# Five forms of the large products, each tried in one block or one chunk

## The chip, the cores and the metric

The kernel runs on one core of a Trainium2 chip. The metric is device time in microseconds (us) from start to end of one launch; less is better. The engines are TensorE (PE, with its weight loads shown apart as PEld), VectorE (DVE), ScalarE (ACT), GpSimd (POOL) and SyncE (SP), which issues most DMAs.

## The reference

Sliding-window attention (8 batches, 8 heads, 576 positions, head size 64, window 128, a linear distance bias), then a feed-forward pair over all 4,608 tokens: 512 to 2,048, Relu, square, 2,048 to 512.

```python
scores = scale * q @ k^T ; where(0 <= rel < 128, scores + bias, -1e9)
attn = exp(scores - max) ; attn / (sum + 1e-9) ; x = attn @ v
h = np.maximum(x @ w_in, 0.0)
return (h * h @ w_out).astype(np.float32)
```

## The kernel before

The 4,608 tokens are cut into `NCH` = 9 chunks of 512. For each chunk `c` the feed-forward part runs over `NF` = 16 slices `f` of 128 hidden units. A slice has two blocks of twelve products: `gemm1(c, f)` writes a [128 hidden x 512 tokens] bank `g`, and `gemm2(c, f)` adds into the four banks `acc[0..3]` ([128 outputs x 512 tokens] each), which are written out after `f` = 15. That is 9 x 16 x 24 = 3,456 large products of 128 x 128 weights by 512 columns.

Precision comes from a split: every f32 operand is kept as a high and a low part of type fp32r, and a product is made of three, high by high, high by low, low by high. The weights of a slice live in one area of 8 KB a partition, in which the high and the low word of a weight lie side by side (`[.., 512, 2]`, line 157). `block` (L177) picks 128 weights of one part, so a plain weight load reads every second word. Where `APART` holds (gemm1, every fourth `f`, first two of four blocks) the order in memory is another one, and the load reads every fourth word. The moving operand of gemm1 is `x[c, p]`, a tile `xu` of [128, 2, 512]: the 512 high words stand together, then the 512 low words. That of gemm2 is `hh` and `hl`, each 512 words together. Every product carries its own weight load.

Behind gemm1 there is a chain per block: ACT Relu out of bank `g` into `r` (L204), DVE square (L207), ACT cast to `hh` (L211), DVE subtraction to `hl` (L213). gemm2 of that slice comes two slices later.

Attention of the later chunks runs in pairs of heads (`Couple`), one pair per four slices: between the blocks TensorE takes the score products (L392, 64-row tiles) and the value products (L338, tiles with 64 columns of weights, into the bank `at`), and `high` and `low` (L477, L480) write the result as the two parts of `xu`. The first chunk's attention (`Wide`, L508, L544, L547) and the conversion of all weights (`convert`, L161: ACT scale, two DVE passes, a cast, a DVE subtraction) fill a prologue of some 37 us and run on into chunk 0.

The order on TensorE is the order of the program: even steps hold gemm1, odd steps gemm2 of two slices before, and the attention pieces stand ahead of every fourth odd step. In the first part a planner (`Plan`) with written costs places all engines' steps; afterwards the engines other than TensorE are ordered by the tile framework, with some steps raised in priority.

Of the kernel before, what the change touches and what calls it, by code (L numbers as in the profile page):

```python
# [9 lines left out]
F32 = mybir.dt.float32  # L10
F32R = mybir.dt.float32r
BF16 = mybir.dt.bfloat16
I32 = mybir.dt.int32
AF = mybir.ActivationFunctionType
ALU = mybir.AluOpType
# [7 lines left out]
NF = DF // 128  # L23
# [14 lines left out]
FIRST = 39  # L38
APART = lambda i, f, b: i == 0 and f % 4 == 0 and b < 2
CASTS = (0, 2, 15,)  # L40
COPIES = (3,)
SQUARES = (6,)
NORMS = (7,)
# [18 lines left out]
class Kern:  # L62
# [98 lines left out]
    def convert(self, f):  # L161
        nc = self.nc
        lo, hi = self.raw[f][..., 0], self.raw[f][..., 1]
        flo, fhi, wl, wh = lo.bitcast(F32), hi.bitcast(F32), self.w[f][..., 0], self.w[f][..., 1]
        nc.scalar.activation(fhi, fhi, AF.Prelu, scale=2.0**-112, alpha=2.0**32)  # L165
        yield
        nc.vector.tensor_scalar(lo, lo, 29, None, op0=ALU.logical_shift_right)
        yield
        nc.vector.scalar_tensor_tensor(lo, hi, 3, lo, op0=ALU.logical_shift_left, op1=ALU.bitwise_or)
        yield  # L170
        (nc.gpsimd.tensor_copy if f in CASTS else nc.scalar.copy)(wh, flo)
        yield
        nc.vector.tensor_tensor(wl, flo, wh.bitcast(F32), op=ALU.subtract)
# [3 lines left out]
    def block(self, i, f, b):  # L177
# [5 lines left out]
            w = w[:, 128 * b : 128 * b + 128]  # L183
        return w[..., 0], w[..., 1]

    def gemm1(self, c, f):
        nc = self.nc
        xs = [self.x[c, p] for p in range(NP)]
        g = self.g1.tile([128, 512], F32, name="g")
        i = 0  # L190
        for cc in range(NCC):
            wl, wh = self.block(0, f, cc)
            for w, part in ((wh, 0), (wh, 1), (wl, 0)):
                nc.tensor.matmul(g, w, xs[cc][:, part], start=i == 0, stop=i == 11)  # L194
                i += 1
                if (c, f, i) == (0, 0, 9):
                    yield
        yield
        r = self.hp.tile([128, 512], F32, name="r", bufs=1)
        hh = self.hp.tile([128, 512], F32R, name="hh")  # L200
        hl = self.hp.tile([128, 512], F32R, name="hl")
        self.h[c, f] = hh, hl
        with self.tc.high_priority(offset=100):
            self.relu = nc.scalar.activation(r, g, AF.Relu)  # L204
        yield
        if c or f in SQUARES:
            nc.vector.tensor_tensor(r, r, r, op=ALU.mult)  # L207
        else:
            nc.scalar.activation(r, r, AF.Square)
        yield  # L210
        nc.scalar.copy(hh, r)  # L211
        yield
        nc.vector.tensor_tensor(hl, r, hh.bitcast(F32), op=ALU.subtract)  # L213

    def gemm2(self, c, f):
        nc = self.nc
        hh, hl = self.h.pop((c, f))
        if f == 0:
            self.acc = self.start_banks if c == 0 else [self.ac.tile([128, 512], F32, name="acc") for _ in range(4)]
        for m in range(4):  # L220
            wl, wh = self.block(1, f, m)
            for i, (w, h) in enumerate(((wh, hh), (wh, hl), (wl, hh))):
                nc.tensor.matmul(  # L223
                    self.acc[m], w, h, start=(f == 0 and i == 0), stop=(f == NF - 1 and i == 2)
                )
            if f == NF - 1:
                o = self.op.tile([128, 512], F32, name="o")
                out = self.outd[m * 128 : m * 128 + 128, 512 * c : 512 * c + 512]
                (nc.scalar.copy if m % 2 else nc.vector.tensor_copy)(o, self.acc[m])  # L229
                (nc.scalar if c == NCH - 1 and m == 3 else nc.sync).dma_start(out, o)  # L230


class Segment:
# [42 lines left out]
    def out(self):  # L276
        (self.nc.vector.tensor_copy if self.k in COPIES else self.nc.scalar.copy)(self.own, self.z)

# [17 lines left out]
    def high(self):  # L296
        K = self.K
        if self.sg == 0:
            K.x[self.c, self.p] = K.xu.tile([128, 2, 512], F32R, name="xu")
        self.u = K.x[self.c, self.p][:, :, 256 * self.sg : 256 * self.sg + 256]  # L300
        self.nc.scalar.copy(self.u[:, 0], self.X)
# [52 lines left out]
class Couple:  # L354
# [118 lines left out]

    def high(self):
        G = self.both[0]
        self.u = self.K.x[G.c, G.p] = self.K.xu.tile([128, 2, 512], F32R, name="xu")
        self.nc.scalar.copy(self.u[:, 0], self.X)  # L477

    def low(self):
# [129 lines left out]
def start(K):  # L609
# [31 lines left out]
    for k in range(8):  # L641
# [12 lines left out]
        P.add(n("z"), "PE", 0.9 * w, (n("n"),) + chain("z"), d - 3, G.turn, ("at", "zp", "pp"), "tw")  # L654
        P.add(n("o"), "DVE" if k in COPIES else "Activation", 0.6, (n("z"),), d - 2, G.out, None, "at")
        P.add(n("m"), "DVE", 0.62 if w == 1 else 0.36, (n("z"),), d + 1, G.also, None, "zp")
# [34 lines left out]
    for f in range(NF):  # L691
        d, last = CONV(f), ("w", f)
        g = K.convert(f)
        for i, (engine, us) in enumerate(CONVERT):
            if i == 3 and f in CASTS:
                engine, us = "Pool", 1.5
# [117 lines left out]
```

## Time and profile before

| | us |
|---|---|
| median of two runs | 956.01 (955.8 and 956.23) |
| span of the profiled execution | 954.1 |
| the two costliest lines on the chain of waits: L223, L194 | 42% of the span each |
| TensorE busy from 446.4 to 549.0 us (about one chunk) | 102.6 of 102.6 |
| TensorE busy from 0 to 37.3 us (prologue) | 34.1 of 37.3 |

Times in the profile are microseconds from the span's start. A row of the timeline holds start, duration, engine, line, operation, what is written from what, the tile on TensorE, the shape and how many were merged; a row of a group ends in busy time, the mean of one in ns, and the idle time ahead of it. Durations of products overlap, so the distance between starts is the time that one takes up.

### The profile page before, as it was taken

How to read it: one execution, taken by the hardware profiler on the slowest of the kernel's cores; microseconds unless marked ns; L12 is line 12 of the kernel's file. 1: busy time of each engine (PE TensorE's matmuls, PEld its weight loads, DVE VectorE, ACT ScalarE, POOL GpSimd, SP SyncE). 2: the span in 40 equal slices, each digit the busy share in tenths (PEclk: the TensorE clock that was granted, in tenths of full speed). 3: DMA queues.
4: the chain of work that ended last, by engine and by line, in shares of the span. 5: the costliest groups of instructions: out<-in, count | busy, mean ns of one | idle time of the engine just before them, and what ended most of it. 6: DMA issues, size and time to landing. Idle time of an engine off the chain costs nothing.

```text
span 954.1 us, 17229 instructions
## 1 busy us (share of the span) xinstructions
PE 945.6 (99%) x6388; PEld 795.7 (83%) x6392; DVE 499.0 (52%) x1334; ACT 417.5 (44%) x1107; POOL 215.3 (23%) x254
## 2 busy tenths in 40 slices
PE   9899999999999999999999999999999999999998
PEld 5688888888888888888888888888888888888886
DVE  6998864455545455444544454455555444433222
ACT  7898743333444444434433343344344343332222
POOL 4123331222222222222222222221212222220000
PEclk9999999999999999999999999999999999999999
DMA  9974423322433333222433232333422231111001
GB/s 348 404 274 153 146 68 119 83 66 66 124 85 83 84 88 107 73 77 73 128 83 83 74 110 72 83 83 92 119 71 72 72 96 45 45 45 45 1 1 44
DMA packets 72883, 95.10 MB, mean 100 GB/s; under 512 B 8032, under 2 KB 41952, under 8 KB 72800
## 3 DMA queue, kind: packets, MB, share of 16 engines
q1 hardware_dynamic: 72368, 93.36, 32.9%
q8 instruction: 50, 0.82, 0.4%
q10 hardware_dynamic: 432, 0.66, 0.2%
q14 instruction: 33, 0.27, 0.1%
HBM read 67.76 MB, written 26.21 MB: 98 GB/s over the span
## 4 chain that ended last, share of the span: by engine, by line
PE 95%; DMA 4%; ACT 0%; issue 0%; DVE 0%; SPq 0%; DVEq 0%
PE acc L223 42%; PE g L194 42%; PE at L338 6%; PE s L392 2%; PE g L392 2%; DMA raw<-in_dram 2%; DMA wide<-in_dram 1%; DMA qk<-in_dram 1%; PE at L392 0%; ACT raw L165 0%; ACT t L426 0%; PE acc L291 0%; ACT t L419 0%; ACT o L229 0%; DVE xu L304 0%
## 5 line engine op out<-in xcount | busy, mean ns | idle before, releaser
L194 PE MATMUL g<-xu,w 128*128 128x512 f32 x1728 | 423.2, 394 | 0.8 <-issue 0.8
L194 PEld LDWEIGHTS g<-xu,w 128*128 128x128 f32 x1728 | 344.1, 209 | 56.2 <-issue 1.7
L223 PE MATMUL acc<-hh,w 128*128 128x512 f32 x1152 | 385.9, 396 | 0.0
L223 PEld LDWEIGHTS acc<-hh,w 128*128 128x128 f32 x1152 | 223.9, 194 | 44.6 <-issue 2.4
L207 DVE TENSOR_TENSOR r<-r 128x512 f32<-128x512 f32 x129 | 104.4, 810 | 245.4 <-ACT r L204 244.2
L204 ACT ACTIVATE r<-g 128x512 f32<-128x512 f32 x144 | 85.9, 597 | 325.8 <-PE g L194 322.7
L223 PE MATMUL acc<-hl,w 128*128 128x512 f32 x576 | 226.6, 393 | 0.0
L326 POOL TENSOR_SCALAR_AFFINE_SELECT pp<-pp 128x512 f32<-128x512 f32 x128 | 107.1, 841 | 210.6 <-DMA pp<-way 171.6
L213 DVE TENSOR_TENSOR hl<-r,hh 128x512 fp32r<-128x512 f32 x144 | 109.4, 760 | 68.3 <-ACT hh L211 67.6
L262 POOL TENSOR_TENSOR t<-t,nm 128x512 f32<-128x512 f32 x64 | 82.8, 1294 | 263.5 <-DVE nm L259 155.9
L223 PEld LDWEIGHTS acc<-hl,w 128*128 128x128 f32 x576 | 112.0, 194 | 19.8
L251 ACT ACTIVATE t<-t,nm 128x128 f32<-128x128 f32 x256 | 100.0, 393 | 56.7 <-DVE nm L244 56.6
L211 ACT CAST hh<-r 128x512 fp32r<-128x512 f32 x144 | 89.0, 618 | 76.1 <-DVE r L207 74.5
L438 DVE COPY_PREDICATED t<-cst,s 64x256 f32<-64x256 int32 x100 | 44.5, 445 | 40.8 <-ACT t L426 22.4
L313 DVE STREAM_TRANSPOSE pp<-t 128x512 f32<-128x512 f32 x64 | 45.2, 707 | 38.7 <-POOL t L262 38.5
L338 PEld LDWEIGHTS at<-pp,v 128*64 128x64 f32 x1024 | 55.2, 137 | 11.2 <-issue 10.8
L338 PE MATMUL at<-pp,v 128*64 128x128 f32 x1024 | 63.0, 276 | 0.0
L244 DVE CUSTOM_DVE_ANT_0 t<-t,cst 128x128 f32<-128x128 f32 x256 | 59.0, 293 | 1.0
L251 ACT ACTIVATION_READ_ACCUMULATOR t<-t,nm 128x1 f32 x256 | 48.2, 188 | 0.0
L392 PE MATMUL s<-qk 64*64 64x64 f32 (+2 forms) x1168 | 46.3, 251 | 0.8 <-ACT raw L165 0.8
L392 PEld LDWEIGHTS s<-qk 64*64 64x64 f32 x1168 | 41.9, 133 | 1.0 <-ACT raw L165 1.0
L428 POOL MEMSET t<- 64x128 f32 (+1 forms) x44 | 9.9, 227 | 137.5 <-PE g L392 128.5
(63 smaller groups left out, 472.2 us busy)
## 6 DMA issues: line engine op xcount, KB each, us to landing
raw<-in_dram SPq DMA_DIRECT2D x32, 512.0 KB, 8.7
way<-pp SPq DMA_DIRECT2D x256, 64.0 KB, 1.8
pp<-way SPq DMA_DIRECT2D x64, 256.0 KB, 2.8
qk<-in_dram SPq DMA_DIRECT2D x32, 320.0 KB, 3.5
v<-in_dram SPq DMA_DIRECT2D x32, 320.0 KB, 2.9
qk<-in_dram SPq DMA_DIRECT2D x38, 256.0 KB, 4.1
out_dram<-o SPq DMA_DIRECT2D x35, 256.0 KB, 4.3
v<-in_dram SPq DMA_DIRECT2D x3, 256.0 KB, 4.9
```

What stands on the lines that cost most here:

```text
L194: nc.tensor.matmul(g, w, xs[cc][:, part], start=i == 0, stop=i == 11)
L204: self.relu = nc.scalar.activation(r, g, AF.Relu)
L207: nc.vector.tensor_tensor(r, r, r, op=ALU.mult)
L211: nc.scalar.copy(hh, r)
L213: nc.vector.tensor_tensor(hl, r, hh.bitcast(F32), op=ALU.subtract)
L223: nc.tensor.matmul(self.acc[m], w, h, start=(f == 0 and i == 0), stop=(f == NF - 1 and i == 2))
L244: self.nc.vector.tensor_tensor_reduce(self.t[:, m], self.t[:, m], self.K.nrel(2 * self.p + m // 2), -0.125, BIG, ALU.add, ALU.min, self.nm ...
L251: return self.nc.scalar.activation(self.t[:, m], self.t[:, m], AF.Exp, bias=nm[:, m : m + 1], scale=-1.0, accum_out=nm[:, 4 + m : 5 + m],)
L262: self.nc.gpsimd.tensor_tensor(self.t, self.t, self.nm[:, 8:12].unsqueeze(2).to_broadcast([128, 4, 128]), op=ALU.mult)
L326: nc.gpsimd.affine_select(to, self.own, pattern=[[-32 * sign, 4], [0, 4], [-sign, 32]], compare_op=op, fill=0.0, base=0, channel_multiplie ...
L338: self.nc.tensor.matmul(self.X[r, o : o + 128].rearrange("p (a c) -> p a c", a=4), v[:, 2 * sg + k, r], src[:, :, 2 * j + i], start=sg == ...
L392: mm = nc.tensor.matmul(to, qk[r, q0 : q0 + 64], qk[r, k0 : k0 + 64 * n], start=True, stop=True, skip_group_check=True,)
```

## The change

Five forms are put into one place each, and the rest stays as it is.

- `CLOSE` = 9: the weights of slice 9 are stored with all high words of a half together and all low words together, so that a load reads 128 words in a row. In `convert` the steps on this slice go through two tiles `o`, as two instructions of 512 elements in place of one of 1,024.
- `NARROW` = 6: in gemm1 of slice 6 each product is made as two of 256 columns.
- `ROWS` = 1: in gemm1 of slice 1 (not in chunk 0) each product is made as two that contract 64 rows each, the first into `g`, the second into a bank of the pool `at`. An ACT copy of `g` and a DVE addition of the other bank come before the Relu.
- `TURNS` = 11: gemm2 of slice 11 takes its products part by part over the four banks, not bank by bank.
- `BESIDE` = 4: in chunk 4 the tile `xu` holds the high and low word of a value side by side, so that the moving operand of gemm1 reads every second word, in all sixteen slices.

```diff
+CLOSE = 9
+NARROW, ROWS, TURNS = 6, 1, 11
+BESIDE = 4
...
+        if f == CLOSE:
+            both = [self.op.tile([128, 512], F32, name="o") for _ in range(2)]
+            for i, o in enumerate(both):
+                nc.vector.scalar_tensor_tensor(
+                    o.bitcast(I32), hi[:, i], 3, lo[:, i], op0=ALU.logical_shift_left, op1=ALU.bitwise_or
+                )
+            yield
+            at = self.arena + f * 8192
+            self.w[f] = nc.alloc_sbuf_tensor_at(f"close{f}", [128, 2, 2, 512], F32R, offset=at).ap().rearrange("p i t d -> p i d t")
+            for i, o in enumerate(both):
+                nc.scalar.copy(self.w[f][:, i, :, 1], o)
+            yield
+            for i, o in enumerate(both):
+                nc.vector.tensor_tensor(self.w[f][:, i, :, 0], o, self.w[f][:, i, :, 1].bitcast(F32), op=ALU.subtract)
+            return
...
+    def product(self, to, w, x, start, stop, narrow=False, other=None):
+        mm = self.nc.tensor.matmul
+        if other is not None:
+            for a, t in ((slice(0, 64), to), (slice(64, 128), other)):
+                mm(t, w[a], x[a], start=start, stop=stop)
+        elif narrow:
+            for a in (slice(0, 256), slice(256, 512)):
+                mm(to[:, a], w, x[:, a], start=start and a.start == 0, stop=stop, skip_group_check=True)
+        else:
+            mm(to, w, x, start=start, stop=stop)
...
+        other = self.at.tile([128, 512], F32, name="at") if c and f == ROWS else None
...
-                nc.tensor.matmul(g, w, xs[cc][:, part], start=i == 0, stop=i == 11)
+                self.product(g, w, xs[cc][:, part], i == 0, i == 11, f == NARROW, other)
...
-            self.relu = nc.scalar.activation(r, g, AF.Relu)
+            if other is not None:
+                nc.scalar.copy(r, g)
+                nc.vector.tensor_tensor(r, r, other, op=ALU.add)
+            self.relu = nc.scalar.activation(r, g if other is None else r, AF.Relu)
...
+        order = [(m, i) for m in range(4) for i in range(3)]
+        if f == TURNS:
+            order.sort(key=lambda y: y[1])
...
     def high(self):
         G = self.both[0]
-        self.u = self.K.x[G.c, G.p] = self.K.xu.tile([128, 2, 512], F32R, name="xu")
+        u = self.K.xu.tile([128, 2, 512], F32R, name="xu")
+        if G.c == BESIDE:
+            u = u.rearrange("p a b -> p (a b)").rearrange("p (n t) -> p t n", t=2)
+        self.u = self.K.x[G.c, G.p] = u
```

On TensorE, gemm1 of slice 1 in chunk 1 was four groups of three products, one group per tile `xu` (`w1_282` are the weights of slice 1):

```order
L194 MATMUL g_1699<-xu_1046,w1_282 128x512 x3
L194 MATMUL g_1699<-xu_1235,w1_282 128x512 x3
L194 MATMUL g_1699<-xu_1457,w1_282 128x512 x3
L194 MATMUL g_1699<-xu_1631,w1_282 128x512 x3
L223 MATMUL acc_102<-hh_1613,w15_946 128x512
```

Now each product stands twice, once into `g` and once into `at`; the first six of the twenty-four:

```order
L208 MATMUL g_1717<-xu_1058,w1_282 128x512
L208 MATMUL at_1718<-xu_1058,w1_282 128x512
L208 MATMUL g_1717<-xu_1058,w1_282 128x512
L208 MATMUL at_1718<-xu_1058,w1_282 128x512
L208 MATMUL g_1717<-xu_1058,w1_282 128x512
L208 MATMUL at_1718<-xu_1058,w1_282 128x512
```

No block changed its place; the number of products in this one went from twelve to twenty-four.

On ACT at the same place (the Relu of slice 1, and the copies of the last chunk's outputs out of two of the `acc` banks) there stood:

```order
L204 ACTIVATE r_1680<-g_1667 128x512
L211 CAST hh_1681<-r_1680 128x512
L204 ACTIVATE r_1712<-g_1699 128x512
L229 COPY o_1728<-acc_103 128x512
L211 CAST hh_1713<-r_1712 128x512
L229 COPY o_1740<-acc_105 128x512
L204 ACTIVATE r_1756<-g_1743 128x512
```

and now:

```order
L237 ACTIVATE r_1698<-g_1685 128x512
L244 CAST hh_1699<-r_1698 128x512
L235 COPY r_1743<-g_1717 128x512
L237 ACTIVATE r_1743<-r_1743 128x512
L264 COPY o_1767<-acc_103 128x512
L264 COPY o_1773<-acc_105 128x512
L244 CAST hh_1744<-r_1743 128x512
L237 ACTIVATE r_1789<-g_1776 128x512
```

A copy was added ahead of the Relu, the Relu waits for DVE's addition, and the cast to `hh` moved behind the second output copy.

More of the change, by code (lines that the diff above doesn't have):

```diff
@@ L219, in gemm2 @@
             self.acc = self.start_banks if c == 0 else [self.ac.tile([128, 512], F32, name="acc") for _ in range(4)]
-        for m in range(4):
[L221 to L225, printed above, removed]
+        order = [(m, i) for m in range(4) for i in range(3)]
+        if f == TURNS:
+            order.sort(key=lambda y: y[1])
+        three = lambda m: [(w, h) for wl, wh in (self.block(1, f, m),) for w, h in ((wh, hh), (wh, hl), (wl, hh))]
+        for m, i in order:
+            w, h = three(m)[i]
+            self.product(self.acc[m], w, h, f == 0 and i == 0, f == NF - 1 and i == 2)
+        for m in range(4):
             if f == NF - 1:
```

## The prediction

> **What bounds the kernel.** I read the busy table, the granted clock and the chain of waits first, then the groups by line:
>
> ```profile
> span 954.1 us, 17229 instructions
> PE 945.6 (99%) x6388; PEld 795.7 (83%) x6392; DVE 499.0 (52%) x1334; ACT 417.5 (44%) x1107; POOL 215.3 (23%) x254
> ...
> PEclk9999999999999999999999999999999999999999
> ...
> PE 95%; DMA 4%; ACT 0%; issue 0%; DVE 0%; SPq 0%; DVEq 0%
> ...
> L194 PE MATMUL g<-xu,w 128*128 128x512 f32 x1728 | 423.2, 394 | 0.8 <-issue 0.8
> L223 PE MATMUL acc<-hh,w 128*128 128x512 f32 x1152 | 385.9, 396 | 0.0
> L223 PE MATMUL acc<-hl,w 128*128 128x512 f32 x576 | 226.6, 393 | 0.0
> ```
>
> TensorE is the bound: busy 99% at the full granted clock, 95% of the chain, and before its 3,456 large products it idles 0.8 us in all. No other engine is over 52%. So a form that makes a product longer is paid in full, and one that makes it shorter is gained in full. The durations in the groups (394 ns) overlap, so they are no price. The price is the distance from start to start, which the timeline of TensorE gives; here a block of twelve products, then one behind an interruption by the 64-column products of attention (line 392):
>
> ```profile
> 503.23 2.92 PE L194 MATMUL g<-xu,w 128*128 128x512 f32 x12
> 505.99 0.39 PE L223 MATMUL acc<-hh,w 128*128 128x512 f32 x1
> ...
> 494.62 0.22 PE L392 MATMUL g<-qk 64*64 64x64 f32 x1
> 494.76 0.51 PE L223 MATMUL acc<-hh,w 128*128 128x512 f32 x1
> 495.11 0.40 PE L223 MATMUL acc<-hl,w 128*128 128x512 f32 x1
> ...
> 497.44 0.40 PE L223 MATMUL acc<-hh,w 128*128 128x512 f32 x1
> ```
>
> (505.99 - 503.23) / 12 = **0.230 us per product**. In the second block the pitch is (497.44 - 495.11) / 10 = 0.233. Its first product shows 0.51 in place of 0.40: nothing ran ahead of it, so its own weight load was not hidden, and that load takes 0.51 - 0.40 = 0.11 us. Within blocks the load lies under the product before.
>
> Now the weight loads. A plain load reads every second word (high and low halves lie side by side); half of the products of gemm1 in every fourth block read every fourth word (APART). The rows are the loads of six APART products, of twelve plain ones, the contiguous 64x128 loads of line 508, then the products of an APART block and the first product of one behind an interruption:
>
> ```profile
> L194 PEld LDWEIGHTS g<-xu,w 128*128 128x128 f32 x6 | 1.5, 309 | 0.0
> ...
> L194 PEld LDWEIGHTS g<-xu,w 128*128 128x128 f32 x12 | 2.3, 194 | 0.4
> ...
> L508 PEld LDWEIGHTS acc<-qk x24: 183/187/333, 6.5 to 14.6; 64*128 64x128 f32 x24
> ...
> 369.47 1.80 PE L194 MATMUL g<-xu,w 128*128 128x512 f32 x7
> ...
> 111.51 0.63 PE L194 MATMUL g<-xu,w 128*128 128x512 f32 x1
> ```
>
> Contiguous 187 ns, every second word 194, every fourth 309. The unhidden parts: 0.11 for every second word, 0.63 - 0.40 = 0.23 for every fourth. In the APART block the seventh product starts at 369.47 + 1.80 - 0.39 = 370.88, so the six before it cost 1.41 / 6 = 0.235 each: the product is now as slow as its load.
>
> This is the row that I build on. 128 weights at every fourth word sweep 2,048 bytes of a partition and take 0.23 us. A moving operand of 512 contiguous words sweeps 2,048 bytes as well and takes 0.230. At every second word the weights sweep 1,024 bytes and take 0.11. It looks as if a read costs by the bytes that it passes over, about 2,048 per 0.23 us, once that is more than the array needs. For comparison, a bf16 product of 512 columns, 1,024 bytes:
>
> ```profile
> 20.99 0.59 PE L121 MATMUL g<-zero 128*128 128x512 bf16 x2
> ...
> 13.57 0.38 PE L121 MATMUL g<-zero 128*128 128x512 bf16 x1
> ```
>
> Its pitch is 0.59 - 0.38 = 0.21. So 0.21 is the array's own time, and 0.230 is a little more than it.
>
> **The change part by part.** *Interleaved moving operand (chunk 4).* All 16 gemm1 blocks of that chunk, 16 x 12 = 192 products, read 512 words at every second place: 4,096 bytes swept. No row shows a moving operand read so. Lower bound 0.230 (nothing changes); upper bound by the weight row at one word per step of 16 bytes, 0.23 / 128 = 1.8 ns a word, 512 x 1.8 = 0.92. By bytes swept it is 2 x 0.230 = 0.46. I take 0.46, since the contiguous product and the every-fourth load already agree on the rate: 192 x 0.230 = **+44.2 us**. [...] The ACT cast and the DVE subtraction that write this layout run once per four blocks, off the path.
>
> *64-row halves (f=1, chunks 1 to 8).* 96 pairs of products, each half contracting 64 rows into its own bank (`g`, `at`). The nearest rows are the 64-row score products of line 508, which go in pairs to two banks, and the change of form from full products to the narrow ones of line 338:
>
> ```profile
> 6.86 1.03 PE L508 MATMUL acc<-qk 64*128 64x256 f32 x8
> 7.82 0.39 PE L121 MATMUL g<-zero 128*128 128x512 bf16 x1
> ...
> L508 PE MATMUL acc<-qk x24: 376/376/480, 6.9 to 14.9; 64*128 64x256 f32 x24
> ...
> 490.72 0.85 PE L194 MATMUL g<-xu,w 128*128 128x512 f32 x3
> 491.50 0.44 PE L338 MATMUL at<-pp,v 128*64 128x128 f32 x4
> ```
>
> The last of the eight starts at 6.86 + 1.03 - 0.38 = 7.51, so three pairs take 0.65, 0.22 a pair. An f32 product of 128 columns alone costs 0.11 (the transposes, below), so one of 256 columns alone is worth 0.22; the pair costs no more, so its two products run at once. Then a pair costs what a product does, 0.230, and the price is the change of form. The last full product starts at 490.72 + 0.85 - 0.39 = 491.18 and would end at 491.41; the narrow ones begin at 491.50: 0.09 of draining, then an unhidden load of 0.11. Into the block and out of it: 2 x 0.20 x 8 = 3.2 us. After an interruption the pitch stayed 0.233 up to the next APART block; with f=1 interrupted that holds for four more blocks, 48 x 0.003 x 8 = 1.2. Together **+4.4 us**; bounds: 0, and 96 x 0.230 + 4.4 = 26.5 if the halves take turns.
>
> *256-column halves (f=6, all nine chunks).* 108 products become 216 with a weight load each. By bytes swept a half takes 0.115, and its load 0.11; the next load starts as the product does. The row for a short product with a load of its own is the transposes:
>
> ```profile
> 15.65 0.60 PE L547 MATMUL acc<-cst,tw 128*128 128x128 f32 x4
> ...
> 23.55 0.49 PE L544 MATMUL at<-cst,tw 128*128 128x128 f32 x3
> 23.88 0.38 PE L547 MATMUL acc<-cst,tw 128*128 128x128 f32 x2
> ```
>
> Two take 0.38, three 0.49, four 0.60: a step of 0.11, so product and load fit into 0.11 together. As the APART products stood 0.005 above their load, I take 0.117 a half, 0.234 a product: 108 x 0.004 = **+0.4 us**. Bounds: 0.21 a product, the array's own time, a gain of 108 x 0.02 = 2; and each half at the full 0.230, +24.8. [...]
>
> *Contiguous weights (f=9).* 9 x 24 products. The load goes from 194 towards 187 ns and lies under a product of 0.230 either way: **0**, at best 216 x (0.230 - 0.21) = -4 if the extra over bf16 came from the weights. In the prologue one DVE pass of 1,024 becomes two of 512:
>
> ```profile
> 87.71 1.51 DVE L173 TENSOR_TENSOR w<-raw,w 128x1024 fp32r<-128x1024 f32 x1
> ...
> 90.98 0.51 PE L194 MATMUL g<-xu,w 128*128 128x512 f32 x1
> ```
>
> The subtraction for f=9 ends at 89.2, its products start at 90.98; two short passes more (some 0.2 us each) fit into 1.8.
>
> *Banks in turn (f=11, gemm2).* gemm1 stays in one bank for twelve products, gemm2 changes it every third, both at 0.230 (503.23 to 505.99 against 494.76 onwards before its 0.233): **0**.
>
> *The added side work of f=1.* Per chunk an ACT copy and a DVE addition stand ahead of the Relu, and ACT copies two outputs before the cast:
>
> ```profile
> 545.57 0.69 DVE L480 TENSOR_TENSOR xu<-at,xu 128x512 fp32r<-128x512 f32 x1
> ...
> 557.48 0.60 ACT L204 ACTIVATE r<-g 128x512 f32<-128x512 f32 x1 [2.87 <-PE g L194]
> ...
> 560.16 0.68 DVE L213 TENSOR_TENSOR hl<-r,hh 128x512 fp32r<-128x512 f32 x1
> ...
> 560.24 0.59 ACT L229 COPY o<-acc 128x512 f32<-128x512 f32 x1
> ...
> 563.00 0.60 ACT L204 ACTIVATE r<-g 128x512 f32<-128x512 f32 x1 [2.17 <-PE g L194]
> ```
>
> The bank `at` is free at 546.3, eight us before f=1 needs it. The chain to `hl` ends at 560.8 today; with 0.6 + 0.7 more and the cast behind the output copy of 560.24 it ends near 562.4, ahead of the next Relu at 563.0, and its gemm2 is four blocks later. Nothing reaches TensorE: **0**.
>
> Sum: 44.2 + 4.4 + 0.4 = 49.0. The profiled span is 954.1; the runs took 955.8 and 956.23, so 1.9 us lie outside the span. 954.1 + 49.0 + 1.9 = **1005 us**.
>
> **The rivals.** (A) *Interleaving is free*: the moving stream has its own path that skips words without cost. Then 956 + 4.8 = 961, not slower. For it: no row shows such a stream. Against it: every-fourth weights cost double. It decides as soon as interleaved products cost under 0.230 + (19 - 5) / 192 = 0.30. (B) *The 64-row halves take turns*, with interleaving doubled: 1005 + 22 = 1027. For it: f32r tiles of that height are not in the trace; against it: the 0.22 a pair. (C) *Interleaving costs part*: the step from 0.11 to 0.23 for weights is a read that waits, and a deeper stream hides half of it: pitch 0.345, 956 + 22 + 5 = 983. (D) *Short products pay their load*: each half 0.230, 1005 + 24.4 = 1029. (E) *Interleaved words are read singly*, 0.92: 1005 + 88 = 1093 and more.
>
> **How the numbers follow.** Forecast 0.56, A 0.18, B 0.10, C 0.10, D 0.03, E 0.03. The predicted time is the forecast's, 1005 (its own range 1000 to 1010 by the bounds of contiguous weights and of the pitch behind an interruption). The range 970 to 1032 takes in B, C and D and those 0.02 of A in which the halves take turns as well (983); it leaves out the rest of A and E, 0.19. Two per cent, about what a measurement of this kernel tells from no change, are 19 us. Slower: forecast, B, C, D, E and 0.02 of A, 0.84, of which I move 0.01 to "same" for a small C: 0.83. Same: 0.16. Faster: all gains together are under 8 us, 0.01.
>
> **What would show it.** In the profile after, the gemm1 products of the fifth chunk at a pitch of 0.46 (0.230 is A, between is C) and that chunk some 44 us longer. The pairs of f=1 at 0.230 with some 0.2 us at each end; f=6 at 0.234 a product; f=9 at 0.230 with loads near 187 ns; f=11 at 0.230. The forecast falls if the moving stream does not follow the weights' rate by bytes swept.

## The result and the profile after

The changed kernel took 1008.94 us (two runs, 1008.6 and 1009.29) against 956.01 before: the ratio is 1.0553, with a 95% interval from 1.0522 to 1.0584. It is slower by 53 us. The span of its profiled execution is 1007.6 us against 954.1, which is 53.5 us more. In its profile the 64-row products are line 208, the 256-column ones line 211, all other large products line 213.

The page of the kernel after: its span, the busy table, the weight loads and the granted clock in 40 slices, the chain by engine, and the two costliest groups.

```profile
span 1007.6 us, 17668 instructions
PE 999.6 (99%) x6596; PEld 809.6 (80%) x6596; DVE 503.5 (50%) x1344; ACT 421.2 (42%) x1116; POOL 216.4 (21%) x254
...
PEld 5688888888888888885675668888888888888887
...
PEclk9999999999999999999999999999999999999999
...
PE 95%; DMA 4%; ACT 0%; issue 0%; SPq 0%
...
L213 PE MATMUL g<-xu,w 128*128 128x512 f32 x1416 | 384.3, 422 | 0.8 <-issue 0.8
L213 PE MATMUL acc<-hh,w 128*128 128x512 f32 x1080 | 359.3, 398 | 0.0
```

TensorE is the bound as before, busy 99% at a granted clock of 1.000 (1.000 before as well), and idles no more than before (0.8 us ahead of the large products). So the 53 us lie inside products. Two rows say where: the mean of the gemm1 group rose from 394 to 422 ns while that of gemm2 went from 396 to 398, and the line of the weight loads has a hollow (567566) in the 19th to 24th of the 40 slices, where the loads stand beside products that last longer. That is some 453 to 605 us, where chunk 4 lies (450.5 to 597.6).

TensorE's timeline after, at one block of each form: the interleaved gemm1 of chunk 4 (12 products) and the row behind it; then, in other chunks, a 64-row block with what stands ahead of it and behind it, the 256-column block, and the block with contiguous weights.

```profile
450.45 5.62 PE L213 MATMUL g<-xu,w 128*128 128x512 f32 x12
455.89 0.42 PE L213 MATMUL acc<-hh,w 128*128 128x512 f32 x1
...
602.92 0.39 PE L213 MATMUL acc<-hh,w 128*128 128x512 f32 x1
603.24 0.51 PE L208 MATMUL g<-xu,w 64*128 64x512 f32 x1
603.24 0.51 PE L208 MATMUL at<-xu,w 64*128 64x512 f32 x1
603.59 0.39 PE L208 MATMUL g<-xu,w 64*128 64x512 f32 x1
...
605.92 0.39 PE L208 MATMUL g<-xu,w 64*128 64x512 f32 x1
605.92 0.39 PE L208 MATMUL at<-xu,w 64*128 64x512 f32 x1
606.25 0.51 PE L213 MATMUL acc<-hh,w 128*128 128x512 f32 x1
...
738.91 3.06 PE L211 MATMUL g<-xu,w 128*128 128x256 f32 x24
741.80 0.40 PE L213 MATMUL acc<-hh,w 128*128 128x512 f32 x1
...
759.27 2.97 PE L213 MATMUL g<-xu,close 128*128 128x512 f32 x12
762.08 0.39 PE L213 MATMUL acc<-hh,w 128*128 128x512 f32 x1
```

The distance between starts, the pitch, gives the price of a product in each form:

- Interleaved: (455.89 - 450.45) / 12 = 0.453 us, about double. The sixteen blocks of chunk 4 lie between 0.451 and 0.471.
- 64-row halves: the two rows of a pair start together; ten pitches from 603.59 to 605.92 are 0.233 each (the pitch that the kernel before showed behind an interruption). Ahead of the first pair 602.92 to 603.24 is 0.32 in place of 0.23 (0.09 of draining), and its own pitch 0.35 (0.11 of weight load); behind the last pair 0.33, and 0.35 again.
- 256-column halves: (741.80 - 738.91) / 24 = 0.120, so 0.241 a product.
- Contiguous weights: (762.08 - 759.27) / 12 = 0.234.

Summed over the blocks of the two traces, the 16 gemm1 blocks of chunk 4 are longer by 43.6 us and all other blocks by 9.5. The work ahead of the first block takes 0.4 more; spans of the kernel before differ by as much among themselves (953.8 to 954.8).

### The profile page after: what moved, and what is told of

It is laid out like the page before. It is cut to its first block, busy times and chain, and to the rows that moved or that the text cites. A ratio compares the mean times of both kernels' runs of the same rounds, so it can differ in the third digit from the quotient of the medians.

```text
span 1007.6 us, 17668 instructions
## 1 busy us (share of the span) xinstructions
PE 999.6 (99%) x6596; PEld 809.6 (80%) x6596; DVE 503.5 (50%) x1344; ACT 421.2 (42%) x1116; POOL 216.4 (21%) x254
## 4 chain that ended last, share of the span: by engine, by line
PE 95%; DMA 4%; ACT 0%; issue 0%; SPq 0%
PE acc L213 41%; PE g L213 39%; PE at L373 6%; PE g L211 3%; PE g L208 3%; PE s L427 2%; PE g L427 2%; DMA raw<-in_dram 2%; DMA wide<-in_dram 1%; DMA cst<-in_dram 1%; PE at L427 0%; ACT raw L168 0%; PE at L208 0%; SPq L143 0%; ACT o L264 0%
## 5 line engine op out<-in xcount | busy, mean ns | idle before, releaser
L213 PE MATMUL g<-xu,w 128*128 128x512 f32 x1416 | 384.3, 422 | 0.8 <-issue 0.8
L213 PE MATMUL acc<-hh,w 128*128 128x512 f32 x1080 | 359.3, 398 | 0.0
L213 PEld LDWEIGHTS g<-xu,w 128*128 128x128 f32 x1416 | 289.0, 215 | 71.1 <-issue 28.9
L213 PEld LDWEIGHTS acc<-hh,w 128*128 128x128 f32 x1080 | 211.4, 196 | 46.6 <-issue 7.9
L237 ACT ACTIVATE r<-g 128x512 f32<-128x512 f32 x136 | 81.1, 596 | 345.0 <-PE g L213 309.0
L213 PE MATMUL acc<-hl,w 128*128 128x512 f32 x540 | 208.5, 394 | 0.0
L213 PEld LDWEIGHTS acc<-hl,w 128*128 128x128 f32 x540 | 105.9, 196 | 20.1 <-issue 2.2
```

What stands on the lines that cost most here:

```text
L213: mm(to, w, x, start=start, stop=stop)
L237: self.relu = nc.scalar.activation(r, g if other is None else r, AF.Relu)
```

## The experiments

Each of the first kernels is the changed kernel with constants set so that only some forms are left (99 is no slice and no chunk).

**The interleaved operand alone, and everything but it.** The first question was whether the forms add up.

```diff
-CLOSE = 9
-NARROW, ROWS, TURNS = 6, 1, 11
+CLOSE = 99
+NARROW, ROWS, TURNS = 99, 99, 99
```

> The kernel before with the interleaved moving operand in chunk 4 alone. If that form is what costs, the time is 956 + 43.5 = about 999.5 us: in the changed kernel the gemm1 blocks of chunk 4 took 43.6 us more than before and those of a chunk without it 0.7 more (43575 ns against 690 to 704), and the gemm2 blocks 0.5 more than those of a like chunk. If part of the 43.6 came from the other four forms lying in the same chunk, it is under 995. The pitch of gemm1 in chunk 4 should be 0.453 to 0.460 us.

Measured: 1000.34 us (4 runs), ratio 1.0463 (1.0448 to 1.0479). The gemm1 blocks of chunk 4 are longer by 43.5 us in all, the gemm2 blocks behind them by 0.8; no other block changed by more than 17 ns. The blocks of chunk 4 are at 0.453 to 0.468, 0.459 on average.

The other half keeps the four small forms:

```diff
-BESIDE = 4
+BESIDE = 99
```

> The changed kernel without the interleaved operand: contiguous weights, 256-column halves, 64-row halves and banks in turn stay. My prediction gave these four +4.8 us (960.9). The trace of the changed kernel, summed over the blocks of the other chunks, gives 8 x about 1.1 us + 0.9, so 965 to 966 us (span near 964). If it lands at 961 the rest belongs to the interleaving.

Measured: 965.41 us, ratio 1.0097 (1.008 to 1.0114). 44.3 and 9.3 make 53.6, against 52.9 for the whole change: the parts add, and the interleaved operand is 83% of it.

**What the interleaving is paid by.** The prediction counted the bytes that a read passes over. Groups of words tell this from a count of pieces: in chunk 2 the high and low words lie in turn, in chunk 4 two high and two low, in chunk 6 four and four. All three pass over 4,096 bytes.

```diff
+GROUP = {2: 1, 4: 2, 6: 4}
...
+        x = self.X
+        if G.c in GROUP:
+            u = u.rearrange("p a b -> p (a b)").rearrange("p (n t j) -> p t n j", t=2, j=GROUP[G.c])
+            x = x.rearrange("p (n j) -> p n j", j=GROUP[G.c])
```

> The kernel before with another layout of the gemm1 operand in three chunks: single words in turn (high, low, high, low) in chunk 2, pairs of words in turn in chunk 4, fours in turn in chunk 6. All three pass over 4,096 bytes for 512 words. Bytes swept (my theory): 0.453 us a product in all three chunks, about 1085 us. Whole 16-byte pieces are read, and a piece that is used fully costs no more than before: 0.453 in chunks 2 and 4, 0.230 in chunk 6, about 1042 us. Pieces of 8 bytes: 0.453, 0.230, 0.230, about 1000 us. Only a step other than one word matters, each jump costing the same: 0.453, about 0.34, about 0.29, about 1031 us.

Measured: 1046.23 us, one run; of the four times expected, 1042 for whole 16-byte pieces is the nearest. The timeline of this kernel at the same block (f=1) of chunks 2, 4 and 6:

```profile
249.92 5.67 PE L213 MATMUL g<-xu,w 128*128 128x512 f32 x12
255.41 0.42 PE L213 MATMUL acc<-hh,w 128*128 128x512 f32 x1
...
499.45 5.67 PE L213 MATMUL g<-xu,w 128*128 128x512 f32 x12
504.95 0.42 PE L213 MATMUL acc<-hh,w 128*128 128x512 f32 x1
...
746.42 2.99 PE L213 MATMUL g<-xu,w 128*128 128x512 f32 x12
749.24 0.40 PE L213 MATMUL acc<-hh,w 128*128 128x512 f32 x1
```

Single words 0.458, pairs 0.458, fours (749.24 - 746.42) / 12 = 0.235. With four words together the price is gone, though the read passes over as many bytes. Bytes passed over are not the cause.

**Streams alone.** The next kernel has no attention and no feed-forward part, only streams of 24 products in one bank, one form after another.

```python
("w1", wt(1), step(x, 1)), ("w4", wt(4), step(x, 1)), ("w8", wt(8), step(x, 1)),
("x2", wt(2), step(x, 2)), ("x4", wt(2), step(x, 4)), ("x8", wt(2), step(x, 8)),
("pairs", wt(2), group(2)), ("quads", wt(2), group(4)),
```

> Leaves out the whole computation: only streams of 24 equal products, one form after the other, so its time stands for nothing. Moving operands of 512 f32r words at a step of 1, 2, 3, 4 and 8 words under plain weights. Bytes swept: 0.230, 0.46, 0.69, 0.92, 1.84 us a product. Distinct 16-byte pieces: 0.230, 0.46, 0.69, 0.92, 0.92. A flat price for any step: 0.230, then 0.46 for all. Weights at a step of 1, 4 and 8 words under a contiguous operand: 0.230 to 0.235, 0.235, and at 8 words 0.235 again if pieces count, 0.46 if bytes swept count. bf16 at a step of 1, 2 and 4 words of two bytes: 0.215, 0.23, 0.46 by bytes or pieces alike (four bf16 at a step of 4 pass over 4,096 bytes), 0.215 for all three if the step is free. Halves of 256 columns with plain and with contiguous weights: 0.115 to 0.121 each; at a step of two words 0.230.

Its timeline, one row a stream: contiguous weights, weights of every fourth and of every eighth word, and the stream behind them; then (weights of every second word) a moving operand of every second, third, fourth and eighth word, in pairs and in fours; and bf16 at steps one and two, with the start of the stream at step four behind; last, halves of 256 columns with weights of every second word, the same with contiguous weights, and the stream behind them.

```profile
12.79 5.61 PE L67 MATMUL odd<-x,w 128*128 128x512 f32 x24
18.24 5.81 PE L67 MATMUL even<-x,w 128*128 128x512 f32 x24
23.88 6.03 PE L67 MATMUL odd<-x,w 128*128 128x512 f32 x24
29.74 5.76 PE L67 MATMUL even<-x,w 128*128 128x512 f32 x24
...
35.34 11.05 PE L67 MATMUL odd<-x,w 128*128 128x512 f32 x24
46.21 11.06 PE L67 MATMUL even<-x,w 128*128 128x512 f32 x24
57.09 11.27 PE L67 MATMUL odd<-x,w 128*128 128x512 f32 x24
68.18 10.53 PE L67 MATMUL even<-x,w 128*128 128x512 f32 x24
78.53 11.07 PE L67 MATMUL odd<-x,w 128*128 128x512 f32 x24
89.42 5.84 PE L67 MATMUL even<-x,w 128*128 128x512 f32 x24
95.10 5.35 PE L67 MATMUL odd<-xb,wb 128*128 128x512 bf16 x23
100.29 5.58 PE L67 MATMUL even<-xb,wb 128*128 128x512 bf16 x24
105.71 1.51 PE L67 MATMUL odd<-xb,wb 128*128 128x512 bf16 x3
...
116.13 3.47 PE L67 MATMUL even<-x,w 128*128 128x256 f32 x24
119.44 3.04 PE L67 MATMUL odd<-x,w 128*128 128x256 f32 x24
122.31 5.68 PE L67 MATMUL even<-x,w 128*128 128x256 f32 x24
```

From start to start over 24 products: step 2 0.453, step 3 0.453, step 4 0.462, step 8 0.431. So a wider step costs no more than a step of two; by bytes passed over, step 8 would have cost 1.84. Pairs 0.454, fours 0.237. bf16 at step 2 is 0.226, near its 0.216 at step 1. Weights of every fourth word give (23.88 - 18.24) / 24 = 0.235 a product, of every eighth (29.74 - 23.88) / 24 = 0.244, where bytes passed over would have made it 0.46; so they are not what weights pay by, either. The contiguous weights give (18.24 - 12.79) / 24 = 0.227, the shortest f32 product of this size seen so far.

**Streams again, with the groups off their place.** Two readings were left: the number of 16-byte pieces touched, or four words in a row in the pattern.

> Leaves out the whole computation: only streams of 24 products, so its time stands for nothing. What fell in the first streams: a step of 2, 3, 4 and 8 words all cost 0.43 to 0.46 us a product, pairs 0.453 too, only fours stayed at 0.237; bf16 at a step of 2 words 0.226, at 4 words 0.452. New theory: the stream runs at full rate while each four words that follow one another lie in one 16-byte piece, and at half rate otherwise, however far the jump. It expects: fours of f32 begun one or two words off such a piece 0.45, eights 0.23 to 0.24, bf16 pairs in turn (four words in 12 bytes) 0.226, bf16 fours in turn 0.22, bf16 at a step of 3 (18 bytes) 0.45. Rival, that four words in a row in the address pattern suffice wherever they begin: fours one or two off 0.237, bf16 pairs 0.45. Weights: contiguous ones gave 0.227 with one weight and one operand repeated, and 0.234 in the changed kernel, where both change from product to product. If the changing operands are the reason, the cycled streams show 0.234 and the single ones 0.227; if the kernel's other engines are, all contiguous streams show 0.227. Plain weights after six products with every-fourth weights: 0.230 if such loads leave the pitch at 0.230, 0.233 otherwise.

Its timeline from 40.18 on: a stream whose first six products have weights of every fourth word and the rest of every second; weights of every second word; fours that begin one word and two words off, and the stream of eights behind them; then bf16 at step 3 (one record of the 24 is missing, one stands apart) and the stream behind it.

```profile
40.18 5.77 PE L73 MATMUL even<-x,w 128*128 128x512 f32 x24
45.79 5.76 PE L73 MATMUL odd<-x,w 128*128 128x512 f32 x24
51.39 11.10 PE L73 MATMUL even<-x,w 128*128 128x512 f32 x24
62.28 11.09 PE L73 MATMUL odd<-x,w 128*128 128x512 f32 x24
73.17 5.79 PE L73 MATMUL even<-x,w 128*128 128x512 f32 x24
...
101.25 7.64 PE L73 MATMUL even<-xb,wb 128*128 128x512 bf16 x22 [0.18 <-issue]
108.73 5.35 PE L73 MATMUL odd<-xb,wb 128*128 128x512 bf16 x24
```

Weights of every second word, with plain moving operands, are at (51.39 - 45.79) / 24 = 0.233 in the streams. Fours that begin one word off their place cost (62.28 - 51.39) / 24 = 0.454, as much as single words, and two words off (73.17 - 62.28) / 24 = 0.454: four in a row is not enough; the fours that lie in one piece of 16 bytes each are the ones at 0.237 above. The theory that it is all or half fell too: bf16 at step 3 takes (108.73 - 101.25) / 22 = 0.340, between the two. What fits every stream is 1.8 ns for each 16-byte piece that a read touches (256 pieces 0.453, 192 pieces 0.340), but not more than some 0.9 ns a word (steps 3, 4 and 8: 0.431 to 0.462 for 512) and not less than the product's own pitch. That is a rule fitted to these rows, not a mechanism that a run isolates.

The same run gave contiguous weights 0.227 whether weights and moving operands changed from product to product or not. So the 0.234 of slice 9 in the kernel is not the price of contiguous weights as such.

**Each of the small forms.** One run left contiguous weights alone (`CLOSE = 9`, the others 99), one took the every-fourth order out of the kernel before, one left the 64-row halves alone.

> The kernel before with contiguous weights of slice 9 alone. My prediction had 0 for it. The changed kernel's trace shows 0.05 us more in gemm1 of slice 9 and 0.04 more in each of seven blocks that follow it up to the next chunk, 0.3 us a chunk: 956 + 2.7 = 958.8 us, a span near 956.8. If the pitch of those blocks came from the other forms, the time is 956 (span 954.2 to 954.5).

Measured: 958.6 us (7 runs) against 955.98, ratio 1.0028 (1.0017 to 1.0039). In chunks 1 to 8 the gemm1 block of f=9 is longer by 49 ns. The four blocks behind it are as before, and the fifth differs by up to 50 ns either way; then, from gemm1 of f=12 to gemm1 of f=15, seven blocks with weights in the old order are longer by 23 to 47 ns each. The order of the blocks fits the place: behind the interruption at f=11 comes gemm2 of f=9, with contiguous weights, and then the every-fourth block of f=12, which used to set the pitch back to 0.230 and here does not. The loads of gemm1 of f=9 in this kernel:

```profile
L213 PEld LDWEIGHTS g<-xu,close 128*128 128x128 f32 x108 | 20.2, 188 | 4.8
```

188 ns a load, as foreseen, and the product is longer all the same.

```diff
-APART = lambda i, f, b: i == 0 and f % 4 == 0 and b < 2
+APART = lambda i, f, b: False
```

> The kernel before with plain weights in all slices, none read at every fourth word. If such a block only costs its own 0.03 us, dropping 36 of them saves 1.1 us (955). If it also sets the pitch back from 0.233 to 0.230 after an interruption, as the traces suggest, all products behind the first interruption run at 0.233: some 24 blocks a chunk x 0.04 x 9 = +8.6 less 1.1, so about 963.5 us (span near 961.6).

Measured: 963.23 us, one run. Without the blocks of every fourth word most blocks run at 0.233, some stretches at 0.230 anyway. So the pitch has two values here, 0.230 and 0.233, that last over many blocks. An interruption sets the longer one, though not always for long: behind the ones at f=15 of chunks 2 and 4 the kernel before is back at 0.230 by the third product. An every-fourth block sets it back, but where contiguous weights stand just ahead of it. The streams don't show this: behind six products of every fourth word, the stream at 40.18 above stays at 0.233.

> The kernel before with the 64-row halves in slice 1 of chunks 1 to 8 alone. Predicted 4.4 us: two changes of form of 0.20 and 0.16 of slower pitch behind them, per chunk. The trace of the changed kernel has 0.087 + 0.265 + 0.147 + 0.040 + 0.040 + 0.046 = 0.62 a chunk, so 956 + 5.0 = 961 us, span near 959.1; inside the block the pairs at 0.230.

Measured: 960.75 us (4 runs), ratio 1.005 (1.0033 to 1.0067). Per chunk: 87 ns on the block ahead, 245 to 265 on the block itself, 147 on the one behind, and 40 to 47 in each of the next three, up to gemm1 of f=3 (the next block but one is the every-fourth block of f=4).

**Contiguous weights in all slices.** Streams said 0.227, slice 9 said 0.234. If the streams are right, all sixteen slices in that order win some 11 us; if slice 9 is, they lose.

```diff
-CLOSE = 9
+CLOSE = range(16)
...
-        if f == CLOSE:
+        if f in CLOSE:
```

> The kernel before with the weights of all sixteen slices in contiguous order (the high words of a half together, the low words together); products, banks and moving operands as before. The blocks of every fourth slice that read another order now read every second word. First theory: in this kernel, contiguous weights run at 0.234 as in slice 9 alone, and nothing sets the pitch back, so all 288 blocks are 40 to 49 ns longer: 11.5 to 14 us, 967 to 970 us, and some more if the longer conversion of the weights holds up the first chunk. Rival: the products of contiguous weights run at 0.2267 as they did alone, and slice 9 was slow only because it stood between slices of the other order: 288 x 12 x 0.0033 = 11.4 us less, 945 us.

> As the kernel with contiguous weights everywhere, but slices 0, 4, 8 and 12, whose first blocks read every fourth word, keep the old order. First theory: the twelve contiguous slices are at 0.234 (216 blocks, 49 ns more each: 10.6 us), the others between 0 and 40 ns more: 966 to 969 us. Rival (contiguous weights run at 0.2267 once their neighbours are contiguous too, or once a block of every fourth word has gone ahead): 216 x 12 x 0.0033 = 8.6 us less in the contiguous slices, 947 us.

Measured: 966.46 and 966.08 us, ratios 1.011 (1.0095 to 1.0125) and 1.0106 (1.0089 to 1.0123). In the kernel, contiguous weights cost some 0.234 everywhere. So something differs between the kernel and the streams: the other engines' work, or the addresses.

> Leaves out the whole computation. Streams of 24 products of 512 columns, each with a weight load, from tiles filled at the start. Seven forms (weights of every second word; six products of every fourth word, then every second; contiguous weights; the same in a larger tile; the same four words further on; the same 60 KB further on; contiguous weights with the moving operand 16 words further on), first with the other engines idle, then once more while ACT copies a bank of PSUM and DVE multiplies out of SBUF all the time. The kernel with contiguous weights everywhere ran at 0.234 a product, the streams with idle engines at 0.2267. First theory: the work of the other engines makes the difference; contiguous streams 0.2267 at first, 0.234 in the second half. Rival: the addresses make it; one or more of the moved forms is at 0.230 or above already in the first half, and the second half repeats the first. If neither shows, the cause lies in what these streams don't have (transfers, the change of banks, the values).

The timeline of this kernel: contiguous weights four words further on, the same 60 KB further on, then the moving operand moved by 64 bytes, and the first stream of the second half; from that half, two of the streams with contiguous weights.

```profile
34.71 5.60 PE L65 MATMUL odd<-x,w 128*128 128x512 f32 x24
40.15 5.60 PE L65 MATMUL even<-x,w 128*128 128x512 f32 x24
45.59 5.68 PE L65 MATMUL odd<-x,w 128*128 128x512 f32 x24
51.11 5.75 PE L65 MATMUL even<-x,w 128*128 128x512 f32 x24
...
73.18 5.60 PE L65 MATMUL even<-x,w 128*128 128x512 f32 x24
78.62 5.60 PE L65 MATMUL odd<-x,w 128*128 128x512 f32 x24
```

The windows of the same run (busy time of PE, PEld, DVE, ACT, POOL, then clock, DMA share and GB/s) show that ACT's work ran in the first half and DVE's in the second; neither half had idle engines, as was meant for the first.

```profile
30.00:45.00 15.00, 15.00 (x68) 12.43 (x67) 0.00 (x0) 13.72 (x25) 0.00 (x0) 1.00 0.42 158
50.00:90.00 40.00, 39.73 (x174) 32.77 (x172) 35.98 (x52) 7.18 (x13) 0.00 (x0) 1.00 0.25 93
```

With ACT at 13.7 of 15 us the contiguous streams are at (40.15 - 34.71) / 24 = 0.227, with DVE at 36 of 40 at (78.62 - 73.18) / 24 = 0.227 as well, and the place of the weights does nothing. Only the moving operand, begun 64 bytes further on, changes the pitch: (51.11 - 45.59) / 24 = 0.230. The first theory fell; the address of the moving operand is what is left. By the sizes of the tiles in the programs (the traces hold no addresses), it begins at a multiple of 128 bytes in the streams. In the kernel every `xu`, `hh` and `hl` begins 32 bytes behind one, because a tile of 4 bytes (`warm`) takes 32 ahead of them.

**The moving operands on the boundary.** The last kernel has contiguous weights everywhere and moves all tiles behind `warm` by 96 bytes.

```diff
-APART = lambda i, f, b: i == 0 and f % 4 == 0 and b < 2
+APART = lambda i, f, b: False
...
-        warm = self.c.tile([128, 1], F32, name="warm")
+        warm = self.c.tile([128, 25], F32, name="warm")[:, 0:1]
```

> The kernel with contiguous weights in all sixteen slices, without the order of every fourth word, and with one small tile (warm) widened from 4 to 100 bytes, so that all tiles behind it, the moving operands xu, hh and hl among them, begin 96 bytes further on: at a multiple of 128 bytes, where those of the streams at 0.2267 began, and not 32 bytes behind one. First theory (a moving operand that begins off such a boundary costs the difference between 0.2267 and 0.234, as the stream moved by 64 bytes hinted with 0.229): 0.2267 a product, 288 blocks x 12 x 0.0033 less 11.4 us, 945 us, faster than both kernels. Rival (the start of the moving operand doesn't matter in the kernel; something else that the streams lack does): 0.234 as before, 966 us.

Measured: 942.44 us (4 runs, 942.23 to 942.72) against 956.36, ratio 0.9856 (0.9839 to 0.9872): faster than the kernel before by 13.9 us, and than the changed one by 66. The first two rows are a block and the row behind it in the kernel with contiguous weights everywhere, off the boundary:

```profile
508.07 2.97 PE L213 MATMUL g<-xu,close 128*128 128x512 f32 x12
510.88 0.39 PE L213 MATMUL acc<-hh,close 128*128 128x512 f32 x1
```

and these the same on the boundary:

```profile
501.58 2.88 PE L213 MATMUL g<-xu,close 128*128 128x512 f32 x12
504.30 0.39 PE L213 MATMUL acc<-hh,close 128*128 128x512 f32 x1
```

2.81 / 12 = 0.234 there, 2.72 / 12 = 0.227 here. In the last kernel 211 of the 288 blocks stand at 226.7 ns a product; the most common pitch of the kernel before is 230.0, in 171 blocks. The blocks some way behind an interruption are at 226.7 too, where the longer pitch lingered before. Two things were edited at once against the kernel with contiguous weights everywhere. Of these `APART` touches the loads of two sub-blocks of four in gemm1 of four slices, which read every second word in that kernel; the one that read every fourth word there was no different (966.08), and the blocks of the other twelve slices changed as well. In the last streams, on the boundary, contiguous weights were at (29.27 - 23.83) / 24 = 0.227 right behind a stream with loads of every fourth and every second word. So the address carries it, as far as these runs go. Not tried: all weights contiguous without `APART` off the boundary, which alone would rule out that those few loads hold all blocks at 0.234; the address alone with the old order of weights (the streams, on the boundary, give 0.233 there, so no gain is in sight); and which boundary it is (the stream begun 64 bytes on was at 0.230, so a multiple of 64 was not enough).

## Why the prediction was right, and where it was not

It said 1005 us and slower; 1008.9 came. The span grew by 53.5 us in place of 49.0. The 4.5 between them are some 2.6 of contiguous weights, 0.8 of 256-column halves, 0.6 of 64-row halves, 0.1 of the interleaved operand and the 0.4 ahead of the first block. By its own steps:

- **What bounds the kernel** (TensorE, every product paid in full): right. The parts add to the whole within 1 us, and no wait appeared.
- **Interleaved operand, +44.2:** alone, measured 43.5 in gemm1 and 0.8 behind it, where the pitch is slower for a few products. The number was right and the reason was wrong; that the number came out was luck. "A read costs by the bytes that it passes over" fell with the fours (same bytes, 0.235) and with step 8 (four times the bytes of step 2, 0.431 against 0.453). The pieces of 16 bytes gave the same number at a step of two words, so the test that the prediction named (a pitch of 0.46) could not tell them apart. The row it leaned on is half a coincidence: weights of every fourth word pay about 1.8 ns a word (0.23 for 128), a moving operand at that step 0.9 (0.462 for 512).
- **64-row halves, +4.4:** alone, measured 5.0 in the trace and 4.8 in the runs. The pairs run at once (0.233 a pair), the change of form costs 0.09 and 0.11 at each end, and the slower pitch lasts up to f=4, all as foreseen. The size was short because the slower pitch (0.233) holds already inside the block of pairs, which the term had at 0.230.
- **256-column halves, +0.4:** measured 9 x 0.132 = 1.2; the term was mis-sized. A half takes 0.1205 us in place of the 0.117 taken. The streams on the boundary gave (122.31 - 119.44) / 24 = 0.120 with contiguous weights. With every second word it is 0.120 by an estimate: the bf16 stream at step 4 ahead of it starts at 105.71 and at 0.452 a product ends at 116.56, and (119.44 - 116.56) / 24 is left. So the load is not what limits a half.
- **Contiguous weights, 0:** this step failed. "The load goes from 194 towards 187 ns and lies under a product of 0.230 either way" was right of the load (188 ns), but the products of that block took 0.234, and seven later blocks of the chunk grew too, some 2.6 us in all. As far as the runs show, what decides is where the moving operand begins, which no row of the kernel before shows. The gain that the prediction allowed for (down to 0.21 a product) is there in part on the boundary: 0.227.
- **Banks in turn, 0:** right of its own. gemm2 of f=11 is some 40 ns longer, and is so too where contiguous weights are the only change.
- **Side work of f=1, 0:** right; no idle time came up ahead of the products.
- **The rivals:** that interleaving is free fell on the pitch of 0.453, that it costs part fell too, and that the 64-row halves take turns fell on pairs whose halves start within 25 ns of each other (4 in the block shown). That short products pay their load (0.230 a half) fell on 0.120, and that interleaved words are read singly (0.92) on 0.453.

## What to carry to other kernels

Where TensorE is the bound, a layout is priced by the distance between the starts of products, not by their mean duration; look at that distance in every block, since a form can slow the blocks behind it that weren't touched (here by 23 to 47 ns in seven blocks behind the contiguous weights of slice 9). Keep the moving operand of f32 products in whole pieces of 16 bytes (four words together in their place took 0.237 us a product in the streams, pairs 0.454), and see where it begins: with contiguous weights, a product took 0.234 us with the operands 32 bytes off a boundary of 128 and 0.227 on it, 3% less. A price that agrees with two rows is still only a number; a pattern that tells its readings apart (here groups of four) is one small run.

## What the runs showed of the hardware

- In the streams a moving operand cost some 1.8 ns for each 16-byte piece, but at most about 0.9 ns a word; that is a rule fitted to their rows (256 pieces 0.453, 192 pieces 0.340, eight words apart 0.431). A product whose weights are every fourth word took 0.235, which is 1.8 ns a weight (309 ns a load), and a load of every second word took 194 ns against 187.
- An f32 product of 512 columns had several pitches, 0.227, 0.230, 0.233 and 0.234 us, that held over many blocks. Off the boundary an interruption (0.233) or contiguous weights (0.234) set a longer one than 0.230; on it, with contiguous weights, 0.227 came back within the block behind an interruption. What keeps the pitch from block to block stays open.
- A 256-column f32 product took 0.120 us against 0.227 to 0.234 for 512, so two halves cost 3 to 6% more than a whole.
